# An adaLN transformer block on one core: all projections over 128 zero-padded rows, LN1 of two blocks by TensorE transposes, FFN weights on GpSimd's DMA queue

## The chip, the cores and the metric

The kernel runs on one core of a Trainium2 chip. The metric is device time in microseconds for one execution; lower is better. All engines of the core (TensorE, VectorE, ScalarE, GpSimd and SyncE, which only issues DMAs here) run their own instruction streams and meet at semaphores.

## The reference, cut to what matters

One sequence of S = 2048 tokens of width D = 448 passes through an attention half and a feed-forward half. Both are wrapped in a layernorm whose scale and shift, and whose output gate, are computed from a condition vector `c`.

```
mod = silu(c) @ w_mod                       # six vectors of 448: sa, ca, ga, sb, cb, gb
h = layernorm(x) * (1 + ca) + sa            # LN1
qkv = h @ wqkv                              # 448 -> 3 x 448; 16 heads of 28
# token s attends to s, s-2, ..., s-14 (8 keys, masked at the start), softmax over them
x = x + ga * (attention @ wo)
h = layernorm(x) * (1 + cb) + sb            # LN2
x = x + gb * ((relu(h @ W_gate) * (h @ W_up)) @ W_down)   # 448 -> 1792 -> 448
```

All tensors are bf16. The number that matters for the change is 448 = 3 x 128 + 64: a contraction over D takes four matmuls, of which the last one has 64 rows of data.

## The kernel before

**Layout.** `x_sb` holds the tokens in 16 tiles of 128 (tokens on partitions). Four blocks of 512 tokens (b = 0 to 3) go through LN1 and the projections. `hT` holds LN1's output transposed: 448 features in four chunks (`cc` or `k`, of `ROWS` = 128, 128, 128 and 64 partitions), tokens along the free dimension. `Wqk` is w_qkv's q and k part with each head of 28 columns padded to 32; `Wv`, `Wg` and `Wu` hold their weights in the same four row chunks.

**LN1.** `ln_stats` takes mean and variance on VectorE, `ln_rstd` makes the factors on ScalarE and VectorE, and `ln_normalize` writes the normalised tile to one of six `hb` buffers. For block 0 (`stage_a0`) VectorE normalises, TensorE transposes the tile in four pieces into PSUM (L527) and ScalarE and VectorE evict it with scale and shift (L538, L540). For blocks 1 to 3 (`stage_a_ln`) GpSimd normalises (L495), SyncE issues one DMA transpose per tile (`ln_transpose`, L502), and GpSimd applies scale and shift in place, one operation per chunk (`ln_affine`, L508). LN2 (`stage_ln2`) goes that second way for all blocks.

**Projections.** `stage_qk` computes eight groups of 128 output columns per block (L571), `stage_v` one group per attention tile of 114 tokens (L599, 18 tiles), `stage_gu` fourteen gate and fourteen up groups per block (L719). Each group is four matmuls that accumulate in one PSUM bank; the fourth contracts over 64 rows:

```
for k in range(4):
    R = ROWS[k]
    last = e.matmul(buf.at, W[0:R, k, 128 * f:128 * f + 128], h2.at[0:R, k, :],
                    start=(k == 0), stop=(k == 3))
```

`stage_down` contracts over F = 1792, in 14 matmuls of 128 rows (L739). In `stage_attn` the logits are matmuls of 28 rows (L626), ScalarE takes the exponential (L640), VectorE multiplies by a 0/1 band mask (L645), and the sum over the keys goes back through TensorE (L654, L662). `stage_y` is the out-projection (L683), four matmuls of 128 rows (the heads' padding included).

**Gates.** The output gates are multiplied into the weights on GpSimd: `wo_pad` in four operations (L761), `Wd` in fourteen (L764).

**Order.** Nothing is ordered by hand. Every step is an `op` with an engine, a cost in ns, what it reads and writes, and a priority (the lower, the earlier). `_Plan.schedule` plays the whole program through once at build time: it takes, engine by engine, the startable operation of the lowest priority number, within a small slack, with all DMA bytes on one line of 250 bytes per ns. The order found is then fixed for every engine and queue; `_semaphores` adds the waits. So an instruction that the plan places too early makes all behind it on its engine wait. Before, LN1 of blocks 1, 2 and 3 has priorities 160, 260 and 360, q/k of the four blocks 50, 150, 300 and 400, the first five attention tiles 200 to 204 on TensorE and 140 to 144 on the other engines, gate/up from 1000.

**Loads.** All but one of the loads are issued by SyncE in order of priority: c, x, the modulation weights, w_qkv (`Wraw`, copied into `Wqk` by VectorE at L424), x, wo, x, and then the FFN weights (4.7 MB with Wd), all before SyncE's first transpose.

Of the kernel before, what the change touches and what calls it, by code (L numbers as in the profile page):

```python
# [5 lines left out]
ACT = mybir.ActivationFunctionType  # L6
# [264 lines left out]
def bass_adaLN_cond__sliding_local_dilated__glu_gated_reglu__prompt_kernel(  # L271
# [15 lines left out]
    with ExitStack() as es:  # L287
# [72 lines left out]
        dma_sems = {SP: [sem(f"dsp{i}") for i in range(64)], ACTE: [sem(f"dact{i}") for i in range(8)]}  # L360
# [10 lines left out]
        op(DVE, 90, lambda e: e.memset(kT[:, :, 0:KOFF], 0.0), w=["kTpad"], prio=-15)  # L371
        hbufs0 = [_Buf(hb_slots) for _ in range(6)]
# [5 lines left out]
        for m, name in ((maskA, "mA"), (maskA0, "mA0")):  # L378
            op(POOL, 200, lambda e, m=m: e.memset(m[:], 0.0), w=[name], prio=-10)
            for o in range(8):  # L380
                op(POOL, 300, lambda e, m=m, o=o: e.affine_select(
                    out=m[:], in_=m[:], compare_op=ALU.not_equal, fill=1.0, base=14 - 2 * o,
                    channel_multiplier=-1, pattern=[[1, NQ]]), r=[name], w=[name], prio=-10)
# [20 lines left out]
        for k in range(4):  # L404
            load(Wraw[0:ROWS[k], k, :], A_wqkv[128 * k:128 * k + ROWS[k], 0:2 * D], [("wraw", k)], ROWS[k] * 2 * D * 2, -7)
# [107 lines left out]
        def stage_a0():  # L513
            for t in range(4):
                ln_stats(t, st, mv, 1, 0)
            ln_rstd(0, 2, mv, lnv, rstd, nmr, 1, 0)
            ln_rstd(2, 4, mv, lnv, rstd, nmr, 1, 0)
# [25 lines left out]

        def stage_a_ln(b, prio):
# [17 lines left out]
        def stage_qk(b, prio):  # L562
            for g in range(4):
                for sec in range(2):
                    buf = _Buf(poolF)

                    def mm(e, g=g, sec=sec, buf=buf):
                        last = None
                        for k in range(4):
                            R = ROWS[k]  # L570
                            last = e.matmul(buf.at, Wqk[0:R, k, 512 * sec + 128 * g:512 * sec + 128 * g + 128], hT[0:R, k, KOFF + TB * b:KOFF + TB * b + TB],  # L571
                                            start=(k == 0), stop=(k == 3))
                        return last
                    op(PE, 4 * _mm(TB), mm, r=[("wqk", k, sec) for k in range(4)] + hT_deps(TB * b, TB * b + TB),
# [16 lines left out]
        def stage_v(t, prio):  # L591
# [259 lines left out]
```

## Time and profile before

| | |
|---|---|
| runs | 306.7 us median of 3 (304.32 to 306.98) |
| profiled execution | 305.23 us; span of its instructions 303.4 us |
| TensorE busy | 265.9 us, 88% of the span; weight loads 95.8 us beside it |
| VectorE, ScalarE, GpSimd busy | 136.2, 120.7 and 71.3 us |
| mean granted TensorE clock | 0.949 of full speed |

The span runs from the first to the last instruction of the profiled execution; the rest of its time lies around that. A TensorE matmul is drawn with a modelled end, so two matmuls in a stream overlap in the picture: the distance from start to start tells what one costs, not its length. PEld is TensorE's loading of weights, which can run beside a matmul. "issue" as a releaser is time in which an engine waited for nothing that the profile shows.

### The profile page before, as it was taken

The numbers are of one execution on the slowest core, as the hardware profiler recorded it, in microseconds if no ns is written. First come the engines' busy times: TensorE is split into PE (matmuls) and PEld (weight loads), VectorE is DVE, ScalarE is ACT, GpSimd is POOL, SyncE is SP. The second block draws the span as 40 slices with busy tenths as digits, with TensorE's granted clock in tenths as the row PEclk, the third lists the DMA queues.
The fourth block names the chain that finished last, engine by engine and source line by source line (L and its number), as shares of the span: only waits on it lengthen the run. The fifth ranks groups of instructions, "written<-read, shape, count | busy, mean of one in ns | idle before, by whom it ended". The sixth has DMA issues, their size and how long they took to land.

```text
span 303.4 us, 4076 instructions
## 1 busy us (share of the span) xinstructions
PE 265.9 (88%) x1594; PEld 95.8 (32%) x1618; DVE 136.2 (45%) x267; ACT 120.7 (40%) x208; POOL 71.3 (23%) x105
## 2 busy tenths in 40 slices
PE   0599655699399999999999999999999999999884
PEld 0323321123123333333444333333433233332232
DVE  6531875203712037666766767743223323223211
ACT  3236763155335566555566566532112221122200
POOL 7403530999501400010250124011040000000000
PEclk9999955599869999999999999999999999999999
DMA  6999993230000000010010300001200000000000
GB/s 178 267 218 312 263 209 70 59 80 2 0 0 17 17 2 0 2 24 13 17 50 16 52 17 19 1 2 36 63 15 17 0 0 15 29 19 0 0 30 31
DMA packets 25003, 16.43 MB, mean 54 GB/s; under 512 B 15960, under 2 KB 23640, under 8 KB 24984
## 3 DMA queue, kind: packets, MB, share of 16 engines
q1 hardware_dynamic: 24712, 15.95, 23.3%
q8 instruction: 12, 0.20, 0.3%
q10 hardware_dynamic: 272, 0.23, 0.2%
q14 instruction: 7, 0.06, 0.1%
HBM read 10.67 MB, written 1.84 MB: 41 GB/s over the span
## 4 chain that ended last, share of the span: by engine, by line
PE 82%; DVE 7%; ACT 3%; DMA 3%; issue 2%; POOL 1%; SPq 0%; ACTq 0%; POOLq 0%
PE psF L719 38%; PE psM L739 15%; PE psF L571 11%; PE psF L599 6%; PE psM L683 5%; DVE EA L645 4%; PE psL L626 3%; DMA bigR<-in_w_mod_dram 3%; PE psM L662 2%; PE psM L654 1%; ACT EA L640 1%; POOL hT L508 1%; DVE o_sb L746 1%; DVE st L477 1%; PE psF L527 1%
## 5 line engine op out<-in xcount | busy, mean ns | idle before, releaser
L725 ACT ACTIVATE g_sb<-psF 128x512 bf16<-128x512 f32 x56 | 33.4, 597 | 80.6 <-PE psF L719 80.2
L727 DVE TENSOR_TENSOR bigR<-psF,g_sb 128x512 bf16<-128x512 f32 x56 | 38.7, 691 | 57.4 <-PE psF L719 56.6
L719 PE MATMUL psF<-h2T,Wu 128*128 128x512 bf16 (+1 forms) x216 | 62.4, 383 | 0.6 <-issue 0.2
L719 PE MATMUL psF<-h2T,Wg 128*128 128x512 bf16 (+1 forms) x213 | 61.6, 383 | 1.4 <-issue 1.3
L739 PE MATMUL psM<-Wd,bigR 128*128 128x448 bf16 x224 | 47.1, 354 | 3.2 <-DVE o_sb L746 2.2
L645 DVE TENSOR_TENSOR EA<-EA,maskA 128x912 bf16<-128x912 bf16 (+1 forms) x36 | 31.0, 860 | 41.1 <-ACT EA L640 40.9
L495 POOL TENSOR_SCALAR hb<-x_sb,rstd,nmr 128x448 bf16<-128x448 bf16 x28 | 20.6, 743 | 116.1 <-DVE nmr L488 113.4
L640 ACT ACTIVATE EA<-psL 128x912 bf16<-128x912 f32 (+1 forms) x36 | 33.2, 922 | 26.6 <-PE psL L626 18.4
L571 PE MATMUL psF<-hT,Wqk 128*128 128x512 bf16 (+1 forms) x123 | 39.8, 435 | 4.0 <-POOL hT L508 1.7
L719 PEld LDWEIGHTS psF<-h2T,Wu 128*128 128x128 bf16 x224 | 18.1, 96 | 41.7 <-issue 27.1
L719 PEld LDWEIGHTS psF<-h2T,Wg 128*128 128x128 bf16 x224 | 17.9, 96 | 40.1 <-issue 28.9
L739 PEld LDWEIGHTS psM<-Wd,bigR 128*128 128x128 bf16 x224 | 19.7, 98 | 24.9 <-DVE o_sb L746 3.7
L746 DVE TENSOR_TENSOR o_sb<-psM,x_sb 128x448 bf16<-128x448 f32 x16 | 10.0, 624 | 27.6 <-PE psM L739 27.4
L477 DVE BATCH_NORM_STATS2 st<-x_sb 128x6 f32<-128x448 bf16 x32 | 19.6, 614 | 4.6 <-DMA x_sb<-in_A_x_dram 4.0
L683 PE MATMUL psM<-wo_pad,qT 128*128 128x448 bf16 x64 | 17.1, 396 | 5.2 <-DVE qT L672 5.2
L571 PEld LDWEIGHTS psF<-hT,Wqk 128*128 128x128 bf16 (+1 forms) x128 | 10.5, 102 | 32.9 <-issue 25.4
L508 POOL TENSOR_SCALAR h2T<-h2T,modc 128x512 bf16<-128x512 bf16 (+1 forms) x16 | 13.8, 860 | 25.2 <-DMA h2T<-hb 24.0
L599 PE MATMUL psF<-Wv,hT 128*128 128x448 bf16 (+1 forms) x72 | 17.8, 358 | 0.0
L626 PE MATMUL psL<-qT,kT 28*128 28x114 bf16 (+1 forms) x288 | 14.2, 220 | 2.8 <-ACT EA L640 2.8
L578 ACT ACTIVATE qT<-psF 128x512 bf16<-128x512 f32 x16 | 9.6, 599 | 13.9 <-PE psF L571 13.9
L764 POOL TENSOR_TENSOR Wd<-Wd,gbc 128x448 bf16<-128x448 bf16 x14 | 14.0, 1023 | 2.1 <-DMA Wd<-in_B_W_down_dram 2.1
L687 DVE TENSOR_TENSOR x_sb<-x_sb,psM 128x448 bf16<-128x448 bf16 x16 | 9.9, 621 | 9.3 <-PE psM L683 8.6
(60 smaller groups left out, 159.7 us busy)
## 6 DMA issues: line engine op xcount, KB each, us to landing
out_dram<-o_sb SPq DMA_DIRECT2D x16, 112.0 KB, 1.7
bigR<-in_w_mod_dram SPq DMA_DIRECT2D x1, 1568.0 KB, 15.9
Wd<-in_B_W_down_dram SPq DMA_DIRECT2D x1, 1568.0 KB, 19.3
x_sb<-in_A_x_dram SPq DMA_DIRECT2D x3, 448.0 KB, 14.7
Wg<-in_B_W_gate_dram SPq DMA_DIRECT2D x1, 1344.0 KB, 17.0
Wu<-in_B_W_up_dram SPq DMA_DIRECT2D x1, 1344.0 KB, 15.9
bigR<-in_w_mod_dram SPq DMA_DIRECT2D x1, 784.0 KB, 8.1
bigR<-in_A_wqkv_dram SPq DMA_DIRECT2D x3, 224.0 KB, 8.2
```

Of the source, the lines that this page charges most:

```text
L477: op(DVE, 600, lambda e: e.bn_stats(stt[:, t, :], x_sb[:, t, :]), r=[("x", t)] + list(extra), w=[(tag, "st", t)], prio=prio)
L495: f = lambda e: e.tensor_scalar(buf.at[:, 0:D], x_sb[:, t, :], rt[:, t:t + 1], nt[:, t:t + 1], ALU.mult, ALU.add)
L571: last = e.matmul(buf.at, Wqk[0:R, k, 512 * sec + 128 * g:512 * sec + 128 * g + 128], hT[0:R, k, KOFF + TB * b:KOFF + TB * b + TB], start= ...
L599: last = e.matmul(buf.at[0:nk, 0:D], hT[0:R, k, KOFF + k0:KOFF + k0 + nk], Wv[0:R, k, :], start=(k == 0), stop=(k == 3))
L626: last = e.matmul(buf.at[0:nk, i, g * NQ:g * NQ + nq], kT[32 * r:32 * r + DH, g, KOFF + k0:KOFF + k0 + nk], qT[32 * r:32 * r + DH, g, s0:s ...
L640: return e.activation(dst, src, ACT.Exp)
L645: return e.tensor_tensor(d, d, msk[0:nk, None, 0:nq].to_broadcast([nk, 8, nq]), ALU.mult)
L683: last = e.matmul(buf.at[:, 0:D], qT[:, g, s0:s0 + 128], wo_pad[:, g, :], start=(g == 0), stop=(g == 3))
L719: last = e.matmul(buf.at, W[0:R, k, 128 * f:128 * f + 128], h2.at[0:R, k, :], start=(k == 0), stop=(k == 3))
L725: op(ACTE, _act(TB), lambda e, gs=gs, gb=bufs[0]: e.activation(gs.at, gb.at, ACT.Relu), r=[bufs[0]], w=[gs], prio=eprio)
L727: op(DVE, _dve(TB), lambda e, gs=gs, ub=bufs[1], f=f: e.tensor_tensor(hh.at[:, f, :], ub.at, gs.at, ALU.mult), r=[bufs[1], gs], w=[hh, (hh ...
L739: last = e.matmul(buf.at[:, 0:D], hh.at[:, f, 128 * j:128 * j + 128], Wd[:, f, :], start=(f == 0), stop=(f == NF - 1))
```

## The change

1. Every matmul of q/k, v, gate and up takes all 128 rows in its fourth chunk too. The upper 64 rows of that chunk are set to zero: in `Wqk`, `Wv`, `Wg` and `Wu` by memsets on VectorE; in `hT` by a memset for blocks 0 and 1 and through the zero padding of `hb` for the DMA transposes.
2. `stage_a0` becomes `stage_a_pe(b, prio, groups)` and serves blocks 0 and 1; block 1's normalisation stays on GpSimd. Blocks 2 and 3 keep DMA transposes (`stage_a_dma`), with priorities 60 and 70 in place of 260 and 360, and a planned size of 450000 bytes per transpose in place of 131072.
3. The five FFN weight loads move from SyncE's queue to GpSimd's, behind a hold: they wait for x tiles 12 to 15 to land and for LN1's factors of tile 7.
4. Smaller: w_qkv's q/k part comes in two loads instead of four; all of x is loaded ahead of the second part of w_mod and of wo; the second mask is copied from the first instead of being built by eight selections; the zeroing of the pad columns of `Wqk` waits for the new memset of its rows.

The core of the diff:

```diff
+        dma_sems = {..., POOL: [sem(f"dpl{i}") for i in range(16)]}
...
+        op(DVE, 350, lambda e: e.memset(hT[64:128, 3, KOFF:KOFF + 2 * TB], 0.0), w=["hT0"], prio=-14)
+        op(DVE, 350, lambda e: e.memset(Wqk[64:128, 3, :], 0.0), w=["wqkz"], prio=-14)
+        op(DVE, 200, lambda e: e.memset(Wv[64:128, 3, :], 0.0), w=["wvz"], prio=-14)
+        op(DVE, 600, lambda e: e.memset(Wg[64:128, 3, :], 0.0), w=["Wgz"], prio=25)
+        op(DVE, 600, lambda e: e.memset(Wu[64:128, 3, :], 0.0), w=["Wuz"], prio=25)
...
-        for k in range(4):
-            load(Wraw[0:ROWS[k], k, :], A_wqkv[128 * k:128 * k + ROWS[k], 0:2 * D], [("wraw", k)], ROWS[k] * 2 * D * 2, -7)
+        load(Wraw[:, 0:3, :], A_wqkv[0:384, 0:2 * D].rearrange("(k p) n -> p k n", p=128),
+             [("wraw", k) for k in range(3)], 384 * 2 * D * 2, -7)
+        load(Wraw[0:64, 3, :], A_wqkv[384:448, 0:2 * D], [("wraw", 3)], 64 * 2 * D * 2, -7)
...
         load_x(4, 8, -6)
-        load(wmod[0:112, :, 2 * D:6 * D], wmod_v[:, :, 2 * D:6 * D], ["wmodB"], D * 4 * D * 2, -5)
+        load_x(8, 12, -5)
+        load_x(12, 16, -5)
+        load(wmod[0:112, :, 2 * D:6 * D], wmod_v[:, :, 2 * D:6 * D], ["wmodB"], D * 4 * D * 2, -4)
...
         def ln_transpose(buf, dst, w, prio):
-            op(SP, 0, lambda e: e.dma_start_transpose(dst(), buf.at), r=[buf], w=w, prio=prio, dma=131072,
+            op(SP, 0, lambda e: e.dma_start_transpose(dst(), buf.at), r=[buf], w=w, prio=prio, dma=450000,
                issue=1250.0)
...
-        def stage_a0():
+        def stage_a_pe(b, prio, groups):
+            t0 = 4 * b
...
+            for j in range(4):
+                hbuf = ln_normalize(t0 + j, rstd, nmr, 1, prio, DVE if b == 0 else POOL)
...
-                        M = ROWS[cc]
-                        last = e.transpose(ps[0:M, cc % 2, 128 * t:128 * t + 128], hbuf.at[:, 128 * cc:128 * cc + M],
+                        last = e.transpose(ps[:, cc % 2, 128 * j:128 * j + 128], hbuf.at[:, 128 * cc:128 * cc + 128],
                                            ident[:])
...
+                op(*((ACTE, 720, fa) if cc < 2 else (DVE, 700, fd)), r=pairs[cc // 2:cc // 2 + 1] + [("mod", 0), ("mod", 4), "hT0"],
+                   w=[("hT", b, cc)], prio=prio)
...
                         for k in range(4):
-                            R = ROWS[k]
-                            last = e.matmul(buf.at, W[0:R, k, 128 * f:128 * f + 128], h2.at[0:R, k, :],
+                            last = e.matmul(buf.at, W[:, k, 128 * f:128 * f + 128], h2.at[:, k, :],
                                             start=(k == 0), stop=(k == 3))
...
-        stage_a0()
+        stage_a_pe(0, 0, ((0, 2), (2, 4)))
         stage_qk(0, 50)
-        for b in (1, 2, 3):
-            stage_a_ln(b, 60 + 100 * b)
+        stage_a_pe(1, 30, ((0, 4),))
+        hold = [("x", 12), (1, "nmr", 7)]
+        load(Wg[:, 0:3, :], B_W_gate[0:384, :].rearrange("(k p) n -> p k n", p=128), ["Wga"], 384 * FF * 2, 45,
+             eng=POOL, issue=1100.0, r=hold)
...
+        load(Wd[:], B_W_down.rearrange("(f p) n -> p f n", p=128), [("Wd", f) for f in range(NF)], FF * D * 2, 46,
+             eng=POOL, issue=1100.0, r=hold)
+        stage_a_dma(2, 60)
+        stage_a_dma(3, 70)
```

`stage_qk` and `stage_v` change their matmuls in the same way as `stage_gu`.

## Rows read from the trace of the kernel before

**Rows 1.** Chain that ended last, the page's part 4, by line

```profile
PE psF L719 38%; PE psM L739 15%; PE psF L571 11%; PE psF L599 6%; PE psM L683 5%; DVE EA L645 4%; PE psL L626 3%; DMA bigR<-in_w_mod_dram 3%; PE psM L662 2%; PE psM L654 1%; ACT EA L640 1%; POOL hT L508 1%; DVE o_sb L746 1%; DVE st L477 1%; PE psF L527 1%
```

**Rows 2.** Windows: length, busy us per engine (x instructions), granted clock, DMA share, GB/s

```profile
30.00:57.60 27.60, 15.10 (x182) 6.68 (x178) 18.56 (x45) 13.99 (x25) 12.07 (x14) 0.63 0.84 161
...
83.00:108.00 25.00, 24.48 (x97) 7.35 (x93) 3.75 (x8) 12.17 (x23) 4.49 (x6) 0.89 0.05 10
108.00:147.00 39.00, 38.26 (x295) 13.51 (x300) 24.70 (x45) 22.86 (x37) 1.41 (x2) 1.00 0.04 8
147.00:207.00 60.00, 58.94 (x461) 22.94 (x468) 40.93 (x80) 33.62 (x58) 14.11 (x16) 1.00 0.12 24
```

**Rows 3.** Timeline, dense gate/up: start us, length us, engine, instruction

```profile
230.39 1.14 PE L719 MATMUL psF<-h2T,Wg 128*128 128x512 bf16 x4
231.47 1.14 PE L719 MATMUL psF<-h2T,Wu 128*128 128x512 bf16 x4
```

**Rows 4.** Timeline of TensorE, v groups around an out-projection group

```profile
88.89 2.00 PE L599 MATMUL psF<-Wv,hT 128*128 128x448 bf16 x8
90.82 0.93 PE L683 MATMUL psM<-wo_pad,qT 128*128 128x448 bf16 x4
91.59 0.73 PE L599 MATMUL psF<-Wv,hT 128*128 128x448 bf16 x3
```

**Rows 5.** Timeline of the tail, one down group of 14 matmuls

```profile
286.91 2.82 PE L739 MATMUL psM<-Wd,bigR 128*128 128x448 bf16 x14 [0.79 <-DVE bigR L727]
```

**Rows 6.** Timeline of weight loads in q/k, idle before and releaser in brackets

```profile
95.22 0.09 PEld L571 LDWEIGHTS psF<-hT,Wqk 64*128 64x128 bf16 x1 [0.42 <-issue]
95.54 0.33 PEld L571 LDWEIGHTS psF<-hT,Wqk 128*128 128x128 bf16 x3 [0.23 <-issue]
```

**Rows 7.** Transposes into hT: issue ns min/median/max, first and last start

```profile
L502 SPq DMA_TRANSPOSE hT<-hb x12: 1190/1268/14957, 25.6 to 64.4; - x12
```

**Rows 8.** Timeline of SyncE's issues

```profile
1.66 0.70 SPq L393 DMA_DIRECT2D bigR<-in_w_mod_dram  x1
...
16.57 6.54 SPq L393 DMA_DIRECT2D Wg<-in_B_W_gate_dram  x2
```

**Rows 9.** Timeline of GpSimd, 15 to 72 us

```profile
24.83 2.81 POOL L495 TENSOR_SCALAR hb<-x_sb,rstd,nmr 128x448 bf16<-128x448 bf16 x4 [12.37 <-DVE nmr L488]
...
52.54 1.41 POOL L495 TENSOR_SCALAR hb<-x_sb,rstd,nmr 128x448 bf16<-128x448 bf16 x2 [7.37 <-DVE nmr L488]
53.94 3.26 POOL L508 TENSOR_SCALAR hT<-hT,modc 128x512 bf16<-128x512 bf16 x4
```

**Rows 10.** Timeline, first q/k matmuls of block 1

```profile
57.65 2.57 PE L571 MATMUL psF<-hT,Wqk 128*128 128x512 bf16 x5 [1.54 <-POOL hT L508]
```

**Rows 11.** Timeline of the start: transposes, q/k of block 0, second x tiles

```profile
11.28 2.11 PE L527 MATMUL psF<-ident,hb 128*128 128x128 bf16 x12
...
15.76 10.18 PE L571 MATMUL psF<-hT,Wqk 128*128 128x512 bf16 x30 [0.22 <-issue]
15.96 0.63 DVE L477 BATCH_NORM_STATS2 st<-x_sb 128x6 f32<-128x448 bf16 x1 [1.36 <-DMA x_sb<-in_A_x_dram]
```

**Rows 12.** Chain in order of time, an attention tile's TensorE parts

```profile
112.93 0.30 PE psL L626 x8
113.23 0.32 PE psM L654 x16
```

**Rows 13.** Timeline of weight loads, block 1's first q/k groups

```profile
58.64 0.10 PEld L571 LDWEIGHTS psF<-hT,Wqk 64*128 64x128 bf16 x1 [0.83 <-issue]
...
60.58 0.10 PEld L571 LDWEIGHTS psF<-hT,Wqk 64*128 64x128 bf16 x1 [0.84 <-issue]
```

**Rows 14.** DMA issues, page's part 6: count, KB each, median us to landing

```profile
Wd<-in_B_W_down_dram SPq DMA_DIRECT2D x1, 1568.0 KB, 19.3
```

**Rows 15.** Timeline, a mask multiply beside GpSimd

```profile
72.92 7.88 DVE L645 TENSOR_TENSOR EA<-EA,maskA 128x912 bf16<-128x912 bf16 x1 [15.28 <-ACT EA L640]
73.35 6.96 POOL L764 TENSOR_TENSOR Wd<-Wd,gbc 128x448 bf16<-128x448 bf16 x7
```

More of the change, by code (lines that the diff above doesn't have):

```diff
@@ L377, in bass_adaLN_cond__sliding_local_dilated__glu_gated_reglu__prompt_kernel @@
         op(DVE, 450, lambda e: e.memset(va4[:, :, :, DH:DH + 1], 1.0), r=["va0"], w=["va1"], prio=20)
[L378 to L383, printed above, removed]
+        op(POOL, 200, lambda e: e.memset(maskA[:], 0.0), w=["mA"], prio=-10)
+        for o in range(8):
+            op(POOL, 410, lambda e, o=o: e.affine_select(
+                out=maskA[:], in_=maskA[:], compare_op=ALU.not_equal, fill=1.0, base=14 - 2 * o,
+                channel_multiplier=-1, pattern=[[1, NQ]]), r=["mA"], w=["mA"], prio=-10)
+        op(POOL, 200, lambda e: e.tensor_copy(maskA0[:], maskA[:]), r=["mA"], w=["mA0"], prio=-9)
         op(POOL, 200, lambda e: e.memset(maskA0[0:14, :], 0.0), r=["mA0"], w=["mA0"], prio=-9)
@@ L510, in ln_affine, with mm @@
             op(POOL, 700, f, r=deps + [("mod", col), ("mod", col + 4)], w=w, prio=prio)
-        def stage_a0():
[L514 to L517, printed above, removed]
+        def stage_a_pe(b, prio, groups):
+            t0 = 4 * b
+            for t in range(t0, t0 + 4):
+                ln_stats(t, st, mv, 1, prio)
+            for ta, tb in groups:
+                ln_rstd(t0 + ta, t0 + tb, mv, lnv, rstd, nmr, 1, prio)
             pairs = [_Buf(poolF) for _ in range(2)]
-            for t in range(4):
-                hbuf = ln_normalize(t, rstd, nmr, 1, 0, DVE)
-                def mm(e, t=t, hbuf=hbuf):
+            for j in range(4):
+                hbuf = ln_normalize(t0 + j, rstd, nmr, 1, prio, DVE if b == 0 else POOL)
+                def mm(e, j=j, hbuf=hbuf):
                     last = None
@@ L569, in mm @@
                         for k in range(4):
-                            R = ROWS[k]
-                            last = e.matmul(buf.at, Wqk[0:R, k, 512 * sec + 128 * g:512 * sec + 128 * g + 128], hT[0:R, k, KOFF + TB * b:KOFF + TB * b + TB],
+                            last = e.matmul(buf.at, Wqk[:, k, 512 * sec + 128 * g:512 * sec + 128 * g + 128], hT[:, k, KOFF + TB * b:KOFF + TB * b + TB],
                                             start=(k == 0), stop=(k == 3))
                         return last
-                    op(PE, 4 * _mm(TB), mm, r=[("wqk", k, sec) for k in range(4)] + hT_deps(TB * b, TB * b + TB),
+                    op(PE, 4 * _mm(TB), mm, r=[("wqk", k, sec) for k in range(4)] + ["wqkz", "hT0"] + hT_deps(TB * b, TB * b + TB),
                        w=[buf], prio=prio, drain=PE_DRAIN)
@@ L597, in mm @@
                 for k in range(4):
-                    R = ROWS[k]
-                    last = e.matmul(buf.at[0:nk, 0:D], hT[0:R, k, KOFF + k0:KOFF + k0 + nk], Wv[0:R, k, :],
+                    last = e.matmul(buf.at[0:nk, 0:D], hT[:, k, KOFF + k0:KOFF + k0 + nk], Wv[:, k, :],
                                     start=(k == 0), stop=(k == 3))
                 return last
-            op(PE, 4 * _mm(D), mm, r=[("wv", k) for k in range(4)] + hT_deps(k0, k0 + nk) + (["hTpad"] if t == 0 else []),
+            op(PE, 4 * _mm(D), mm, r=[("wv", k) for k in range(4)] + ["wvz", "hT0"] + hT_deps(k0, k0 + nk) + (["hTpad"] if t == 0 else []),
                w=[buf], prio=prio, drain=PE_DRAIN)
@@ L710, in stage_gu @@
                 bufs = []
-                for W, names in ((Wg, ["Wga", "Wgb"]), (Wu, ["Wua", "Wub"])):
+                for W, names in ((Wg, ["Wga", "Wgb", "Wgz"]), (Wu, ["Wua", "Wub", "Wuz"])):
                     buf = _Buf(poolF)
```

33 lines of the change are left out of this document (13 added, 20 removed).

## The prediction

> **What bounds the kernel now.** I read the chain of work that ended last first. Its largest parts are TensorE's: gate and up (L719) 38% of the span, down (L739) 15%, the q/k projections (L571) 11%, v (L599) 6% [rows 1]. Then the windows by stage, to see where TensorE idles. From 83 us on it doesn't: 24.5 busy of 25.0, 38.3 of 39.0, 58.9 of 60.0, while VectorE and ScalarE are never above 69% [rows 2]. Every nanosecond taken off a TensorE instruction there is taken off the end. The one weak stage is 30 to 57.6 us: 15.1 busy of 27.6, granted clock 0.63 [rows 2].
>
> Third I asked whether busy means fast. In the dense gate/up stretch a group of four 512-column matmuls starts every 1.07 us (230.39, then 231.47) [rows 3]. For 448 columns the trace has a direct pair: two v groups, whose fourth matmul has 64 rows, take 1.93 us (88.89 to 90.82), 0.965 a group; the out-projection group behind them, four matmuls of 448 columns with 128 rows each, takes 0.77 (90.82 to 91.59) [rows 4]. Same columns, same stretch, 0.195 us apart. The down projection, 128 rows throughout, runs 14 matmuls in 2.82 us [rows 5]; less the last one's drawn length of about 0.35 (the out-projection's four, drawn to 0.93, make way after 0.77, so a drawn matmul overhangs its slot by 0.16) and over 13 spacings, that is 0.19 each. So 128-row matmuls of 448 columns cost 0.19; 64 more columns at 2.4 GHz add 0.027, an estimate: 0.218 for 512, 0.87 a group against the 1.07 seen. The weight loads show where the 0.20 sits: the 64-row load starts only after 0.42 us of idle, and the 128-row load behind it after another 0.23, both put down to "issue" [rows 6]. Going from 128 rows to 64 and back each costs about 0.10.
>
> **Part 1: full rows.** Removed: two switches in each of 32 q/k, 18 v and 112 gate/up groups; nothing is added on TensorE, as the matmul length follows the columns. 162 x 0.20 = 32.4 us. Subtract the cases in which the next thing is a 28-row logit burst anyway: 18 tiles x 2 bursts, nearly all behind a projection, so some 32 x 0.10 = 3.2. **Gain 29**, all of it on a bound engine but for block 0's 12 groups (2.4). Cover that could fail: from 108 to 207 us VectorE is busy 65.6 of 99 us [rows 2]; that stretch holds about 56 gate/up groups, and without 56 x 0.20 the same work is 75% of it. It holds on average; I allow up to 5 lost.
>
> The Trainium skill (TensorE: Matmul & The Clock Gate, The mechanism) says that a weight load overlaps matmuls in flight only when its row group differs. By that, a stream of nothing but 128-row matmuls would hide no load. This trace disagrees: 128-row down matmuls follow each other every 0.19 us with their loads hidden [rows 5]. What it would do here is the last of the rivals.
>
> **Part 2: block 1's LN1.** Before, block 1 is late for reasons outside its arithmetic. Its first DMA transpose sat 14.96 us in SyncE's issue (the longest of the twelve) [rows 7], queued behind the weight loads, whose gate pair took 6.54 us to issue [rows 8]. And its four scalings on GpSimd stand behind a normalisation for block 0's second LN, which waited 7.37 us; they start at 53.94 [rows 9], and q/k of block 1 waits for them until 57.65 [rows 10]. After, TensorE transposes and ScalarE/VectorE evictions replace both. Before, the statistics of x tiles 4 to 7 began at 15.96, when the tiles landed [rows 11]; 3 us of those, 2.8 of normalising [rows 9] and the transposes end near 24, under block 0's q/k, which last until 25.9 [rows 11]. So block 1's eight q/k groups and four v groups run from about 26 to 36 instead of from 57.65.
>
> What that is worth: from 36 to about 58 the attention tiles over blocks 0 and 1 are all that TensorE has, paced by their own chain. I keep that stretch as holey as before, since blocks 2 and 3 still go through DMA transposes and GpSimd scalings. At 58 us, beyond what was done at 57.65, there are then 8 x 0.87 + 4 x 0.77 = 10.0 us of projections, and two more tiles, each 2 x 0.30 logits and 0.32 AV [rows 12], one matmul of 456 columns (0.19) and 0.77 of out-projection [rows 4]: 3.8. **Gain 13.8**; bounds 0 (block 2 later by as much) and 26.3 (the 12.5 us of idle in that window filled too). Added: four transpose groups at 2.11/3 = 0.70 [rows 11], **cost 2.8** in the dense part; below it 0, if they fall into gaps of q/k.
>
> Cold clock: block 1's first two groups are 1.94 apart (64-row loads at 58.64 and 60.58) [rows 13] against 1.07, behind the window with granted clock 0.63; another stretch like it follows after 83. With q/k of block 1 straight behind block 0, one of the two goes: **gain 1.7**, bounds 0 and 3.5.
>
> **Part 3: the loads.** Five weight loads go from SyncE's queue to GpSimd's, held until x tile 12 has landed and block 1's statistics are done (about 20 us). Queued behind them on GpSimd: the normalisations of blocks 2 and 3, the scalings, the wo and Wd multiplications; TensorE waits for these through q/k of block 2. The weights themselves are wanted by the first gate/up, which came behind q/k and v of block 3 before and may come some 40 us earlier after; some 20 us of landing (Wd took 19.3 [rows 14]) puts them at 40 to 45, so transfer time costs nothing. No load on this queue is in the trace. One issue on SyncE spans 0.70 us on an empty queue [rows 8] to 15 on a full one [rows 7]; GpSimd's queue starts empty, so I take the short end, doubled for an engine not seen at it, 7 us in all, which the attention tiles from 36 us on cover. Bounds: 0 (a gain is excluded, since issuing is work added to GpSimd), and 5 x 15 = 75 us of a blocked GpSimd (a rival). On SyncE the transposes of blocks 2 and 3 no longer stand behind those loads: that is what keeps block 2 near 58. The Trainium skill (SBUF — State Buffer, SBUF: two separate sides) says that descriptors of loads on GpSimd's queue wait while VectorE holds a port that the two share; no run here shows it.
>
> Wd's scaling: one VectorE mask multiply took 7.88 us at 72.92, and ended when GpSimd's seven back-to-back Wd multiplications (73.35 to 80.31) did [rows 15]; TensorE idled about 5 us. All fourteen multiplications stay, at other times: 0 taken, bounds -5.1 and +9 (all fourteen in a row beside the attention).
>
> At nothing: the second mask by copy (GpSimd idles from 12.5 to 24.8), two w_qkv issues fewer, the load order (wmodA ends the start either way), five VectorE memsets, which fill gaps of the start while VectorE waits for x and TensorE for wmodA; without that cover 2.1, by the costs the diff gives them (0.35, 0.35, 0.2, 0.6, 0.6).
>
> **The sum.** The profiled execution is 305.2 us, span 303.4 and 1.8 around it, 0.5% under the median of 306.7. 303.4 - 29.2 - 13.8 + 2.8 - 1.7 = 261.5, with the 1.8 **263.3: 263 us**.
>
> **Rivals.**
> - *The early hole closes.* TensorE has no idle in that stretch: 263 - 12.5 = 250. For it: work of block 1 is there early. Against: with only attention to do, TensorE waited on the tiles' own chain before as well: 15.1 busy of 27.6.
> - *The hole moves.* Block 2 inherits block 1's place: GpSimd busy with issues, transposes beside the weight loads. Part 2 gives nothing: 263 + 13.8 = 277. For it: the old order had the same flaw, and the order written by the planner assumes costs of its own.
> - *Zero rows don't remove the gap* (it belongs to psF's eviction or the accumulation group): 305.2 - 13.8 + 2.8 - 1.7 = 292.5. Against: v and y, side by side [rows 4].
> - *Slower: GpSimd's queue blocks.* If each of five issues holds GpSimd for X, block 2's q/k start at 20 + 5X + 11.6 (normalise 2.8, transposes about 5, scaling 3.3, 0.5). What followed q/k of block 2 took 303.4 - 83 = 220.4; less 27.6 of switches and four tiles done ahead (7.5), 185.3. It turns slower when block 2 starts after 305.2 - 1.8 - 185.3 = 118, so from X = 17.3. With X = 20, a third above the longest issue seen: 131.6 + 185.3 + 1.8 = 319. Against: those 15 us came from a full queue.
> - *Loads of full-row weights can't hide behind a full-row matmul.* Then every matmul pays its load, 0.11 (three in 0.33) [rows 6]: 4 x (0.218 + 0.11) = 1.31 a group, 0.24 more than now. 263 + 29 + 162 x 0.24 = 331. Against: the down matmuls [rows 5]. (The Trainium skill's sentence cited in part 1 would have it so.)
>
> **How the numbers follow.** Forecast 0.56 (254 to 272); hole closes 0.17; hole moves 0.18; zero rows useless 0.04; queue blocks 0.04; loads that can't hide 0.01. The range takes in the forecast, most of the first two rivals, 249 to 281. Only the last two rivals are slower: 0.05; within 1%, about what a measurement of this kernel can tell from no change, nearly nothing.
>
> **What would show it.** Step 1: gate/up groups 0.87 apart, no 64-row loads, L719 spacing equal per column to L739's. Step 2: block 1's q/k within 2 us of block 0's. Step 3: short issues on GpSimd's queue, weights landed by 50, block 2's q/k by 60. I am wrong if groups stay at 1.07, if TensorE's holes between 36 and 60 are much over 12 us or vanish, or if the faster projections leave TensorE waiting on VectorE between 100 and 190.

## The result and the profile after

The changed kernel takes **264.5 us** (median of 3, 264.21 to 264.88) against 306.7 before: a ratio of 0.8645, interval 0.858 to 0.871. The forecast was 263. Its profiled execution has a span of 262.4 us, 41.0 shorter than before. The total came out as forecast. The experiments below show that the early hole (part 2) and the stall beside `Wd`'s scaling did not, and that these two errors cancelled.

First the chain that ended last, by line, which answers to [rows 1]. Line numbers have moved: q/k is L570, v L597, gate/up L716, down L736, the mask multiply L643.

```profile
PE psF L716 36%; PE psM L736 16%; PE psF L570 11%; PE psF L597 4%; PE psM L681 3%; POOL Wd L771 3%; PE psL L624 3%; DVE EA L643 2%; PE psM L652 2%; DVE st L479 1%; POOL hT L510 1%; DVE o_sb L743 1%; ACT EA L638 1%; POOL wo_pad L768 1%; DVE qT L670 1%
```

The mask multiply has gone from 4% to 2%, and `Wd`'s scaling on GpSimd (L771, 3%) is new. The windows by stage, with the columns of [rows 2]:

```profile
28.00:39.40 11.40, 11.24 (x89) 5.81 (x86) 2.59 (x6) 8.39 (x16) 4.94 (x7) 1.00 1.03 361
39.40:60.00 20.60, 11.55 (x147) 5.14 (x148) 13.61 (x19) 11.20 (x16) 18.70 (x18) 0.68 0.42 65
...
90.40:123.00 32.60, 32.03 (x296) 14.96 (x303) 24.93 (x48) 21.82 (x38) 3.46 (x4) 1.00 0.06 13
```

TensorE is still full from 90 us on, and there is still one weak stage: 39.4 to 60, with 9.05 us of idle and a granted clock of 0.68 (another 4.0 us of idle lie between 60 and 90.4). Before, that stage was 30 to 57.6 with 12.5 idle; it now comes behind block 1's projections instead of ahead of them. The timeline of TensorE, cut to projections, out-projections and one of the four transpose groups (L529), with the lines between left out, against [rows 10] and [rows 11]:

```profile
23.64 0.39 PE L529 MATMUL psF<-ident,hb 128*128 128x128 bf16 x4
23.87 1.03 PE L570 MATMUL psF<-hT,Wqk 128*128 128x512 bf16 x4
29.50 6.85 PE L570 MATMUL psF<-hT,Wqk 128*128 128x512 bf16 x31 [0.16 <-issue]
36.19 3.19 PE L597 MATMUL psF<-Wv,hT 128*128 128x448 bf16 x16
50.90 1.68 PE L681 MATMUL psM<-wo_pad,qT 128*128 128x448 bf16 x4 [2.51 <-DVE qT L670]
57.05 1.67 PE L681 MATMUL psM<-wo_pad,qT 128*128 128x448 bf16 x4 [1.80 <-DVE qT L670]
60.05 1.11 PE L570 MATMUL psF<-hT,Wqk 128*128 128x512 bf16 x3 [0.33 <-POOL Wd L771]
```

Block 1's q/k starts at 29.50 instead of 57.65, and block 2's at 60.05. Dense gate/up (against [rows 3]): groups start 0.865 us apart (the next one stands at 202.20), where they were 1.07 apart.

```profile
200.48 1.03 PE L716 MATMUL psF<-h2T,Wu 128*128 128x512 bf16 x4
201.34 1.03 PE L716 MATMUL psF<-h2T,Wg 128*128 128x512 bf16 x4
```

GpSimd (against [rows 9]): the five weight loads are issued in 3.9 us. Behind them come the normalisations of blocks 2 and 3, `wo`, `Wd` and block 2's scaling.

```profile
24.46 1.51 POOL L399 DMA_DIRECT2D Wg<-in_B_W_gate_dram  x2
...
27.27 1.11 POOL L399 DMA_DIRECT2D Wd<-in_B_W_down_dram  x1
...
51.86 3.00 POOL L771 TENSOR_TENSOR Wd<-Wd,gbc 128x448 bf16<-128x448 bf16 x3
54.85 3.90 POOL L510 TENSOR_SCALAR hT<-hT,modc 128x512 bf16<-128x512 bf16 x4
```

Of the transposes into `hT`, eight are left on SyncE (issue in ns, minimum, median, maximum; against [rows 7]), and `Wd` lands in 14.1 us instead of 19.3 [rows 14]. Last, the mask multiply: its longest was 7.88 us [rows 15], and it is now 1.65.

```profile
L504 SPq DMA_TRANSPOSE hT<-hb x8: 1190/1272/6113, 29.2 to 51.9; - x8
```

```profile
Wd<-in_B_W_down_dram POOLq DMA_DIRECT2D x1, 1568.0 KB, 14.1
```

```profile
L643 DVE TENSOR_TENSOR EA<-EA,maskA x36: 585/632/1652, 30.0 to 161.6; 128x912 bf16<-128x912 bf16 x34, 124x880 bf16<-124x880 bf16 x2
```

That last row is the first sign of a term that the forecast had put at 0: the stall beside `Wd`'s scaling.

### The profile page after: what moved, and what is told of

It is laid out like the page before. It is cut to its first block, busy times and chain, and to the rows that moved or that the text cites. A ratio compares the mean times of both kernels' runs of the same rounds, so it can differ in the third digit from the quotient of the medians.

```text
span 262.4 us, 4091 instructions
## 1 busy us (share of the span) xinstructions
PE 229.6 (88%) x1609; PEld 109.4 (42%) x1634; DVE 140.9 (54%) x277; ACT 120.2 (46%) x207; POOL 73.5 (28%) x98
## 4 chain that ended last, share of the span: by engine, by line
PE 76%; DVE 11%; POOL 6%; issue 3%; ACT 2%
PE psF L716 36%; PE psM L736 16%; PE psF L570 11%; PE psF L597 4%; PE psM L681 3%; POOL Wd L771 3%; PE psL L624 3%; DVE EA L643 2%; PE psM L652 2%; DVE st L479 1%; POOL hT L510 1%; DVE o_sb L743 1%; ACT EA L638 1%; POOL wo_pad L768 1%; DVE qT L670 1%
## 5 line engine op out<-in xcount | busy, mean ns | idle before, releaser
L724 DVE TENSOR_TENSOR bigR<-psF,g_sb 128x512 bf16<-128x512 f32 x56 | 38.7, 690 | 43.2 <-PE psF L716 39.4
L716 PE MATMUL psF<-h2T,Wu 128*128 128x512 bf16 x215 | 55.9, 379 | 0.8 <-issue 0.5
L716 PE MATMUL psF<-h2T,Wg 128*128 128x512 bf16 x213 | 55.7, 379 | 1.0 <-issue 0.6
L736 PE MATMUL psM<-Wd,bigR 128*128 128x448 bf16 x224 | 47.1, 353 | 3.6 <-DVE o_sb L743 2.6
L643 DVE TENSOR_TENSOR EA<-EA,maskA 128x912 bf16<-128x912 bf16 (+1 forms) x36 | 27.3, 758 | 18.5 <-ACT EA L638 18.3
L716 PEld LDWEIGHTS psF<-h2T,Wu 128*128 128x128 bf16 x224 | 21.3, 98 | 24.9
L736 PEld LDWEIGHTS psM<-Wd,bigR 128*128 128x128 bf16 x224 | 21.0, 98 | 25.6 <-DVE o_sb L743 4.0
L570 PE MATMUL psF<-hT,Wqk 128*128 128x512 bf16 x123 | 30.3, 400 | 0.8 <-POOL Wd L771 0.3
L716 PEld LDWEIGHTS psF<-h2T,Wg 128*128 128x128 bf16 x224 | 21.0, 98 | 23.8
L570 PEld LDWEIGHTS psF<-hT,Wqk 128*128 128x128 bf16 x128 | 12.9, 103 | 16.3 <-issue 3.4
L597 PE MATMUL psF<-Wv,hT 128*128 128x448 bf16 (+1 forms) x72 | 15.7, 365 | 1.6 <-DVE hT L540 1.6
L624 PEld LDWEIGHTS psL<-qT,kT 28*128 28x128 bf16 (+1 forms) x288 | 8.3, 98 | 16.9 <-ACT EA L638 7.4
L771 POOL TENSOR_TENSOR Wd<-Wd,gbc 128x448 bf16<-128x448 bf16 x14 | 14.6, 1067 | 0.0
L665 ACT ACTIVATE lnD<-psM 128x456 f32<-128x456 f32 x18 | 9.9, 550 | 7.6 <-PE psM L660 7.6
## 6 DMA issues: line engine op xcount, KB each, us to landing
Wd<-in_B_W_down_dram POOLq DMA_DIRECT2D x1, 1568.0 KB, 14.1
```

Of the source, the lines that this page charges most:

```text
L570: last = e.matmul(buf.at, Wqk[:, k, 512 * sec + 128 * g:512 * sec + 128 * g + 128], hT[:, k, KOFF + TB * b:KOFF + TB * b + TB], start=(k = ...
L597: last = e.matmul(buf.at[0:nk, 0:D], hT[:, k, KOFF + k0:KOFF + k0 + nk], Wv[:, k, :], start=(k == 0), stop=(k == 3))
L624: last = e.matmul(buf.at[0:nk, i, g * NQ:g * NQ + nq], kT[32 * r:32 * r + DH, g, KOFF + k0:KOFF + k0 + nk], qT[32 * r:32 * r + DH, g, s0:s ...
L643: return e.tensor_tensor(d, d, msk[0:nk, None, 0:nq].to_broadcast([nk, 8, nq]), ALU.mult)
L716: last = e.matmul(buf.at, W[:, k, 128 * f:128 * f + 128], h2.at[:, k, :], start=(k == 0), stop=(k == 3))
L724: op(DVE, _dve(TB), lambda e, gs=gs, ub=bufs[1], f=f: e.tensor_tensor(hh.at[:, f, :], ub.at, gs.at, ALU.mult), r=[bufs[1], gs], w=[hh, (hh ...
```

## The experiments

The theory: full rows save two switches of row count a group; block 1's projections ahead of the hole save the rest; the loads' new queue gives nothing. The rivals: the gain belongs to something else in the new order, a 64-row matmul is slow in itself, the loads' queue is what counts, or the stall at the mask multiply is. Ratios are to the kernel before, run on the same chip as each experiment (medians 305.0 to 305.7 us there).

### e1 and e2: the rows alone, and all but the rows

e1 is the kernel before with full rows and the memsets that zero them, and nothing else:

```diff
+        op(DVE, 600, lambda e: e.memset(Wg[64:128, 3, :], 0.0), w=["Wgz"], prio=25)
...
-                            last = e.matmul(buf.at, W[0:R, k, 128 * f:128 * f + 128], h2.at[0:R, k, :],
+                            last = e.matmul(buf.at, W[:, k, 128 * f:128 * f + 128], h2.at[:, k, :],
```

> The kernel before with the zero rows alone (part 1 of the prediction), nothing else of the change. If going from 128-row to 64-row matmuls and back costs 0.10 us each time, 162 groups lose 0.20 each less some 3 us beside logits: 305.2 - 29 = 276 us, and gate/up groups start every 0.87 us. If the gap belongs to the accumulation group or to the bank's eviction, groups stay at 1.07 and the time at 305.

Measured: 277.2 us (276.7 to 277.8), ratio 0.907 [0.897, 0.918]: 27.8 us less than before. In the same trace v and the out-projection, 448 columns each and 0.195 apart in [rows 4], now cost the same: two v groups in 1.51 us, then 0.76 a group.

```profile
86.21 1.68 PE L604 MATMUL psF<-Wv,hT 128*128 128x448 bf16 x8
87.72 0.92 PE L688 MATMUL psM<-wo_pad,qT 128*128 128x448 bf16 x4
88.48 2.43 PE L604 MATMUL psF<-Wv,hT 128*128 128x448 bf16 x12
```

But the stall of [rows 15] stayed and grew. The mask multiply took 9.86 us, up to the end of GpSimd's run, and TensorE waited 7.90 (one line of each engine):

```profile
70.13 9.86 DVE L650 TENSOR_TENSOR EA<-EA,maskA 128x912 bf16<-128x912 bf16 x1 [12.56 <-ACT EA L645]
72.55 6.95 POOL L769 TENSOR_TENSOR Wd<-Wd,gbc 128x448 bf16<-128x448 bf16 x7
81.74 0.57 PE L659 MATMUL psM<-EA,vaug 128*32 128x114 bf16 x16 [7.90 <-DVE EA L650]
```

e2 goes the other way: the kernel after, every engine's order unchanged, with 64 rows back in the fourth matmul of q/k, v and gate/up.

```diff
-                            last = e.matmul(buf.at, W[:, k, 128 * f:128 * f + 128], h2.at[:, k, :],
+                            last = e.matmul(buf.at, W[0:ROWS[k], k, 128 * f:128 * f + 128], h2.at[0:ROWS[k], k, :],
```

> The changed kernel with 64-row fourth matmuls put back in q/k, v, gate and up; the order on every engine is the same. If part 1 adds to the rest: 264.5 + 29 = 293 us. If the early stages now hide the gaps (attention paced), 5 less: 288. If the rows don't matter, 264.5.

Measured: 298.1 us, ratio 0.976 [0.965, 0.987], 33.6 above the kernel after, and the groups are 1.07 apart again:

```profile
196.19 1.14 PE L716 MATMUL psF<-h2T,Wu 128*128 128x512 bf16 x4
197.26 1.14 PE L716 MATMUL psF<-h2T,Wg 128*128 128x512 bf16 x4
```

So the rows are worth 27.8 us in the old order and 33.6 in the new one, and everything else 7.0 without full rows and 12.7 with them.

### e3 and e4: a slow matmul, or a switch of row count?

Zero rows could help because a 64-row matmul is slow, or because changing the row count is. In e3 all gate/up matmuls have 64 rows (rows 0 to 63 of each chunk, so half of the contraction is left out). In e4 only gate and up have their 64-row fourths back, and up goes through its chunks as 3, 0, 1, 2: 64-row matmuls stand in pairs, and each group has one switch instead of two.

```diff
-                            last = e.matmul(buf.at, W[:, k, 128 * f:128 * f + 128], h2.at[:, k, :],
+                            last = e.matmul(buf.at, W[0:64, k, 128 * f:128 * f + 128], h2.at[0:64, k, :],
```

```diff
-                        for k in range(4):
+                        ks = (0, 1, 2, 3) if W is Wg else (3, 0, 1, 2)
+                        for k in ks:
+                            R = ROWS[k]
```

> The changed kernel, but every gate/up matmul contracts over rows 0 to 63 of its chunk (half of the contraction is left out), in the same order. If the cost is in the change of the row count, the groups still start every 0.87 us and only the borders to 128-row work pay, some 80 x 0.10 = 8: 265 to 273 us. If a 64-row matmul is slow in itself, 0.20 for each, 448 x 0.20 less what hides: far over 300 us.

> The changed kernel with 64-row fourth matmuls in gate and up alone, but up takes its chunks in the order 3, 0, 1, 2, so that the two 64-row matmuls of a pair stand side by side. If a switch costs 0.10, two in a pair remain of four: 56 x 2 x 0.10 = 11 us more than the changed kernel, 276 us, and a pair takes 1.94. If each 64-row matmul costs 0.20 wherever it stands: 112 x 0.20 = 22 more, 287 us.

e4: 279.2 us (279.06 to 279.34), ratio 0.914 [0.904, 0.924]. Groups start 0.97 us apart (the next one stands at 207.50), halfway between 0.865 and 1.07, and the trace of weight loads shows where: after a load of one size, the load of the other size comes only after 0.42 us of idle; the second 64-row load of a pair follows the first at once.

```profile
205.57 1.13 PE L718 MATMUL psF<-h2T,Wg 128*128 128x512 bf16 x4
206.54 1.13 PE L718 MATMUL psF<-h2T,Wu 64*128 64x512 bf16 x4
```

```profile
206.31 0.09 PEld L718 LDWEIGHTS psF<-h2T,Wg 64*128 64x128 bf16 x1 [0.42 <-issue]
206.32 0.10 PEld L718 LDWEIGHTS psF<-h2T,Wu 64*128 64x128 bf16 x1
206.84 0.33 PEld L718 LDWEIGHTS psF<-h2T,Wu 128*128 128x128 bf16 x3 [0.42 <-issue]
```

One switch is therefore worth (1.07 - 0.865) / 2 = 0.1025 us. In time, that is 112 x 0.1025 = 11.5 of the 14.7 us that e4 lies above the kernel after. Another 1.3 us are two groups that e4 ran at the lower clock, from 90.38 to 93.65, where the kernel after kept the full one; the remaining 1.9 were not traced.

e3: 301.4 us, where the switch theory had 265 to 273 and the slow matmul far over 300. The total alone would speak for the slow matmul; the spacing does not. At full clock e3's groups are 0.87 apart (220.03, then 220.90), as with 128 rows: a 64-row matmul is not slow in itself, which is what the run was for. The time went elsewhere:

```profile
220.03 1.03 PE L716 MATMUL psF<-h2T,Wg 64*128 64x512 bf16 x4
220.90 1.02 PE L716 MATMUL psF<-h2T,Wu 64*128 64x512 bf16 x4
```

```profile
90.00:120.00 30.00, 29.70 (x154) 10.04 (x149) 13.07 (x25) 11.69 (x18) 0.00 (x0) 0.51 0.00 1
120.00:150.00 30.00, 30.00 (x128) 9.68 (x127) 11.50 (x23) 10.51 (x19) 4.27 (x6) 0.50 0.09 18
```

These are the windows from 90 to 150 us: TensorE is drawn busy throughout and its granted clock is 0.51 and 0.50, the lower of its two levels (1.2 GHz). The kernel after has 1.00 over the same stretch. Neither theory had this in it.

### e5 and e6: the loads' queue, and block 1's transposes

e5 issues the five weight loads from SyncE, behind the same hold; e6 sends block 1 through DMA transposes and GpSimd scalings again, at the same priority.

```diff
-             eng=POOL, issue=1100.0, r=hold)
+             r=hold)
```

```diff
-        stage_a_pe(1, 30, ((0, 4),))
+        stage_a_dma(1, 30)
```

> The changed kernel with the five FFN weight loads issued by SyncE again, behind the same hold; the order of the compute engines is the same. If the queue matters as part 3 said, the transposes of blocks 2 and 3 sit behind those loads again (one issue of some 15 us) and q/k of block 2 slips from 60 us by 5 to 10: 270 to 275 us. If the transposes wait for the same DMA engines on either queue, or GpSimd's own work sets block 2 in any case: 264 to 266.

> The changed kernel with block 1's LN1 by DMA transposes and GpSimd scalings (its new priority 30 kept), so without TensorE's transposes for it. If block 1's early arrival is worth what part 2 said, 12.7 us net: 277 us. If the early stretch is paced by attention and by block 2 either way, 3 or less: 264 to 267.

e5: 265.3 us (264.6 to 266.4), ratio 0.869 [0.863, 0.874], against 0.8645 [0.858, 0.871] after: no difference that the runs can tell. The transposes' longest issue is back at 14.2 us, yet block 2's scaling starts at 53.70 rather than 54.85: GpSimd was busy with its own multiplications until then in either case.

```profile
L504 SPq DMA_TRANSPOSE hT<-hb x8: 1189/1266/14172, 24.8 to 50.8; - x8
```

```profile
50.71 3.01 POOL L771 TENSOR_TENSOR Wd<-Wd,gbc 128x448 bf16<-128x448 bf16 x3
53.70 3.90 POOL L510 TENSOR_SCALAR hT<-hT,modc 128x512 bf16<-128x512 bf16 x4
```

e6: 275.6 us (274.3 to 278.2), ratio 0.903 [0.896, 0.911], 11 above the kernel after, as part 2 had it, but not by part 2 alone. Block 1's q/k starts at 47.58 (18 us later than after, 10 earlier than before), and a mask multiply of 7.51 us is back, beside another GpSimd run. How the 11 us divide between the two was not measured:

```profile
47.08 7.51 DVE L643 TENSOR_TENSOR EA<-EA,maskA 128x912 bf16<-128x912 bf16 x1
47.58 6.19 PE L570 MATMUL psF<-hT,Wqk 128*128 128x512 bf16 x16
47.70 2.02 POOL L771 TENSOR_TENSOR Wd<-Wd,gbc 128x448 bf16<-128x448 bf16 x2
```

### e9 and e10: the stall by itself

To price the stall, `Wd`'s fourteen multiplications are made to wait for attention tiles 5 to 9, three to a tile, so that they no longer run in a row early on. e9 does this to e1 (old order, full rows), e10 to the kernel after.

```diff
-               r=[("Wd", f), ("gbc", 1)], w=[("Wds", f)], prio=900)
+               r=[("Wd", f), ("gbc", 1), ("on", 5 + f // 3)], w=[("Wds", f)], prio=900)
```

> The kernel before with zero rows (277.2 us) and one thing more: GpSimd's fourteen Wd multiplications wait for attention tiles 5 to 9, three per tile, instead of running as soon as GpSimd is free. If VectorE's one mask multiply of 9.9 us (TensorE idle 7.9 us behind it) comes from that run of multiplications, the stall goes and the time falls to 269 to 271 us. If the stall has another cause, 277.

> The changed kernel with the same spreading of the Wd multiplications. Six of them (6.4 us) stood ahead of block 2's scalings on GpSimd between 46 and 55 us. If they hold q/k of block 2, that starts some 6 us earlier than 60 and the time falls to 259 to 261 us. If attention's own chain paces the stretch, 264; if the multiplications now slow VectorE beside gate/up, 266.

e9: 270.5 us (270.1 to 272.2), ratio 0.886 [0.881, 0.892], 6.7 below e1. The longest mask multiply is 1.32 us, and from 70 to 85 us TensorE is busy 15.00 of 15.00, where e1 has 7.10. So the stall came from those multiplications running in a row.

e10: 262.4 us (261.4 to 263.9), ratio 0.858 [0.852, 0.864], between the two expectations. Block 2's scaling starts at 48.42, 6.4 us earlier; q/k of block 2 at 59.39, only 0.7 earlier. Out-projections, block 1's projections and the first ones behind the hole, in e9 and then in e10 (lines between left out):

```profile
42.26 1.67 PE L688 MATMUL psM<-wo_pad,qT 128*128 128x448 bf16 x4 [1.69 <-DVE qT L677]
48.29 1.67 PE L688 MATMUL psM<-wo_pad,qT 128*128 128x448 bf16 x4 [1.69 <-DVE qT L677]
54.33 1.68 PE L688 MATMUL psM<-wo_pad,qT 128*128 128x448 bf16 x4 [1.69 <-DVE qT L677]
57.15 9.31 PE L576 MATMUL psF<-hT,Wqk 128*128 128x512 bf16 x32 [1.14 <-POOL hT L513]
66.29 3.19 PE L604 MATMUL psF<-Wv,hT 128*128 128x448 bf16 x16
```

```profile
29.77 7.08 PE L570 MATMUL psF<-hT,Wqk 128*128 128x512 bf16 x32
36.69 3.19 PE L597 MATMUL psF<-Wv,hT 128*128 128x448 bf16 x16
50.76 1.67 PE L681 MATMUL psM<-wo_pad,qT 128*128 128x448 bf16 x4 [1.69 <-DVE qT L670]
56.79 1.67 PE L681 MATMUL psM<-wo_pad,qT 128*128 128x448 bf16 x4 [1.69 <-DVE qT L670]
59.39 1.72 PE L570 MATMUL psF<-hT,Wqk 128*128 128x512 bf16 x4
```

Out-projections come every 6.03 us in both, each behind 1.69 us of waiting for the same VectorE result. With block 1's projections ahead of them the first comes 8.5 us later (50.76 against 42.26), and the spacing is the same. That suggested that the hole is paced by attention's own chain from tile to tile, whatever GpSimd does. TensorE's lower clock may be part of that pace: from 50.76 to 56.79 e10's granted clock is 0.50, and TensorE is idle for 2.2 of the 6.03 us (waits of 0.53 and 1.69), so that a tile's work takes it 3.8, where the prediction's rows, at the full clock, have 1.88. No run has these tiles at the full clock.

### e11 and e12: what paces the hole?

e11 is e10 with TensorE's order changed (a lower planned size for the DMA transposes, 300000, puts the first q/k group of block 2 ahead of the second out-projection). e12 is e10 with `wo`'s modulation row asked for earlier, so that GpSimd scales `wo` in time in which it waited (the diffs show what differs from e10). e14 is the kernel after again, on the same chip.

```diff
-            op(SP, 0, lambda e: e.dma_start_transpose(dst(), buf.at), r=[buf], w=w, prio=prio, dma=450000,
+            op(SP, 0, lambda e: e.dma_start_transpose(dst(), buf.at), r=[buf], w=w, prio=prio, dma=300000,
```

```diff
-        mod_row(0, 2, 231)
+        mod_row(0, 2, 100)
```

> The kernel after with the Wd multiplies spread (as in e10, 262.4 us), and with the planner's cost of a DMA transpose, which only orders the program, lowered from 450000 to 300000: TensorE's written order then has the first q/k group of block 2 ahead of the second out-projection, instead of behind it and the next attention tile. If the order at the hole's end costs the 6 us by which block 2's scaling became earlier in e10 without q/k following: q/k of block 2 at 52 to 54 us instead of 59.4, and 257 to 260 us. If attention's chain (6.0 us from one out-projection to the next, 50.76 to 56.79 in e10) paces TensorE whatever stands beside it: the q/k groups only fill its gaps, q/k of block 2 is done at most 1 to 2 us earlier, and 261 to 262.5 us.

> The kernel after with the Wd multiplies spread, and with the modulation row that scales the output projection's weight asked for earlier (priority 100 instead of 231), so that GpSimd multiplies wo at about 31 us, in time in which it waited (8.3 us before 41.8 in e10), instead of at 41.8 to 46.7. If GpSimd's work before block 2's scaling is what still holds the hole open: scaling 4 to 5 us earlier than 48.4, q/k of block 2 at 53 to 55, 257 to 260 us. If attention's chain paces it: first out-projection still at 50 to 51 us, q/k of block 2 at 57 to 59, 261 to 263 us.

> The kernel after, unchanged, beside the two others on one chip: 264 to 265 us by every theory. It shows whether the 2 us between it and e10 (262.4) are more than the difference of two chips.

e11: 261.9 us (261.4 to 263.4). e12: 263.0 (261.8 to 263.6). e14: 265.3 (264.0 to 266.5). Attention's chain held in both. In e11 the q/k group does stand at 53.74, but it only fills the 1.69 us that TensorE waited ahead of the second out-projection, and the two keep their 6.04 us; in e12 block 2's scaling starts at 44.51, another 3.9 us earlier, and q/k of block 2 only 0.5 us earlier, at 58.91.

e11 moved one group only; no run puts more of block 2's groups among the tiles. The traces bound what that could give with these tiles: once block 2's scaling is done, TensorE waits 2.2 us before q/k of block 2 in e10 (0.53 and 1.69, from 52.47 on) and 3.9 in e12 (twice 1.69 and 0.53, from 48.04 on).

```profile
49.60 1.67 PE L681 MATMUL psM<-wo_pad,qT 128*128 128x448 bf16 x4 [1.69 <-DVE qT L670]
53.74 1.91 PE L570 MATMUL psF<-hT,Wqk 128*128 128x512 bf16 x4
55.64 1.68 PE L681 MATMUL psM<-wo_pad,qT 128*128 128x448 bf16 x4
```

```profile
44.51 3.53 POOL L510 TENSOR_SCALAR hT<-hT,modc 128x512 bf16<-128x512 bf16 x4 [1.06 <-DMA hT<-hb]
```

Spread multiplications are thus worth 2 to 3 us in the kernel after: on one chip, e11 lies 3.4 below e14 (ratios 0.861 [0.857, 0.866] and 0.871 [0.867, 0.876]) and e12 2.3 (0.863 [0.858, 0.868], an interval that just overlaps e14's). Both have a second edit, and e10, which has none, ran on another chip with an interval that overlaps the kernel after's; so the size is rough. e10, e11 and e12 are the fastest versions, and the runs can't tell them apart.

## Why the prediction was right, point by point

The runs make a path from before (305.1 us beside them) to after; the forecast's terms stand beside it. The third step lumps block 1's transposes with the new order, the loads and the smaller edits: only the loads were taken out by themselves (e5), and block 1's transposes only with the stall coming back (e6).

| step | time, us | change | forecast |
|---|---|---|---|
| before | 305.1 | | |
| full rows (e1) | 277.2 | -27.8 | -29.2 |
| `Wd` multiplications out of the way (e9) | 270.5 | -6.7 | 0 |
| block 1 by TensorE, order, loads (e10) | 262.4 | -8.1 | -12.7 (-13.8, +2.8, -1.7) |
| `Wd` multiplications back, in the new order (after) | 264.5 | +2.1 | 0 |
| together | | -40.5 | -41.9 |

**Part 1 held**, in mechanism and in size: gate/up groups 0.865 (forecast 0.87), a switch 0.10, and no sign of VectorE as the new bound: in e1 TensorE is busy all of 147 to 207 us (60.00 of 60.00), part of the stretch that the forecast had asked about. In e1 the saving on TensorE was partly eaten: TensorE's wait at the stall went from 5.08 to 7.90 us. In the new order, without the stall, the rows give 33.6, near the 32.4 of 162 groups before the logit bursts are taken off. Rows of zeros cost nothing that shows: 448 columns take 0.76 us a group in v and in the out-projection alike. The Trainium skill (TensorE: Matmul & The Clock Gate, Back-to-back issue gap) has the isolated gap of matmuls at full clock follow from the columns alone; the spacing here (0.865 / 4 = 0.216 us for 512 columns, with 64 rows in e3 or 128) agrees; the lower figure that it gives for a sustained stream, 131 ns, was not reached in any stretch read here.

**Part 2 was mis-sized**: "two more tiles" (3.8 us) was wrong, and wrong in sign. The step reasoned that a stretch as holey as before, from 36 to 58, would take the attention tiles 22 us on; but 22 us at the old pace hold fewer tiles than the 27.6 us of before, and no row stood for two more. The hole is paced by attention's chain, 6.03 us from tile to tile, and but for a first logit burst that chain starts only when block 1's v is done, since TensorE's order has the projections first: at 39.4, not at 36, with the first out-projection at 50.90. When q/k of block 2 begins there are two out-projections done where e9 has three.

What remains between e9 and e10 is the 10.0 us of projections moved, less the 2.2 by which block 2's q/k starts later than block 1's did (59.39 against 57.15), less 0.7 of attention work left over (one out-projection of 0.77 and one matmul of 456 columns, 0.19, fewer; one logit burst of 0.30 more); and 1.4 us of cold clock, against 1.7 forecast: behind the hole, at the lower clock, block 1's q/k takes 9.1 us in e9 (57.15 to 66.29), where it takes 6.9 in e10, and of those 2.2 us e10 pays 0.8 in its first group of block 2 (1.65 from 59.39 to the logit burst at 61.04, against 0.87). Those together are 8.5, close to the 8.1 between e9 and e10.

Two smaller readings of that step were off as well. Block 1's q/k was to follow block 0's within 2 us; it came 4.8 us behind (29.50 against 24.73), because three of block 0's v groups, a logit burst and a run of small matmuls for the modulation stand between them, which the step left out. And a transpose group costs 0.22 us in the dense stream (23.64 to 23.87), 0.9 for the four, where 2.8 had been taken from the 0.70 of [rows 11].

**Part 3: the size held, the reason failed.** Moving the loads costs and gives nothing that the runs can tell (e5). The issues took 0.55 to 1.1 us each, 3.9 in all against 7 forecast, so the rival of a blocked GpSimd is out, and the weights were there at about 42 us. But "that is what keeps block 2 near 58" is not so: with the loads back on SyncE and one transpose's issue at 14.2 us, block 2 starts no later. What the Trainium skill says of descriptors that wait while VectorE holds the shared port (SBUF — State Buffer, SBUF: two separate sides), cited in the prediction, did not show as a late landing: `Wd` landed in 14.1 us from GpSimd's queue and 19.8 from SyncE's in e5.

**The stall was the term put at 0.** The prediction saw it [rows 15], noted 5 us of TensorE idle, and took 0 because all fourteen multiplications stay. Its own lower bound, -5.1, was near: 6.7 saved and 2.1 given back (2.3 to 3.4 beside e14), 4.6 net. That made good the 4.6 missing in part 2. The forecast's mechanism held for part 1, by far the largest term; that the total came within 1.5 us is luck in the other two.

Of the rivals, "the hole closes" would have needed more of TensorE's other work among the tiles, which block 2's late scaling did not allow; "the hole moves" was half right, since the hole did move behind block 1, but it took only 4.6 us of part 2; zero rows useless, a blocked queue and loads that can't hide are out by e1, e2 and the traces (groups 0.865 apart, issues of at most 1.1 us).

## What to carry to other kernels

Compare the cost per column of matmuls whose neighbours differ in row count: where the count changes within an accumulation group, each change cost 0.10 us here, and a memset of zero rows took all of it away. A hole that an engine's work falls into may be paced by its own dependence chain; then work put ahead of it delays the chain (the first out-projection by 8.5 us here), and the tiles behind it keep their spacing. Count the gain as the work moved, less the delay at the hole's end and the tiles that no longer fit, not as idle time filled. When a stall of one engine coincides with a run of another, ask what the new order does to that coincidence before writing 0: here it was 6.7 us.

## What the hardware showed that was not expected

A TensorE that is drawn busy without a gap ran at the lower clock: in e3 the granted clock was 0.51 and 0.50 through 60 us (90 to 150) with 59.7 us drawn busy, in a stretch of half-height (64-row) gate/up matmuls and attention tiles, while the same order with 128 rows had 1.00. The clock fell at about 91 us, behind TensorE waits of 1.15, 0.29 and 0.29 us. It fell there in e4 and e10 too, and was back at 1.00 by 94; the kernel after has the same waits and kept 1.00. In e3 it came back only at about 159 us, behind the first seven 128-row down matmuls of the stretch. From 180 us on e3 has 1.00 with the same half-height matmuls, so height alone does not decide; no run here tells what does.

A mask multiply of 0.63 us took 7.51 to 9.86 us beside a run of GpSimd operations of 0.7 to 1.0 us each (before, e1, e6), until the run ended. The Trainium skill (SBUF — State Buffer, Who interferes with whom) has the shared port pair as a lock that an engine gets for one whole instruction while the other waits; a wait through up to ten instructions is more than that. Nor is a long run enough: in the kernel after GpSimd is busy from 46.1 to 60.7 without a break, its operations stretched to as much as 1.3 us, and no mask multiply took over 1.65. What decides which engine gives way was not found.
